# Rounding in small matrix chains on ScalarE, a shorter denominator, three subtractions by transfer, and a new order of the program

## The chip, the core and the metric

The kernel runs on one core of one Trainium2 chip. The metric is the device time of one execution in microseconds (us). The engines are TensorE (PE, with its weight loads shown apart as PEld), VectorE (DVE), ScalarE (ACT), GpSimd (POOL) and SyncE (SP, which here only issues DMAs). Each engine works through its own instructions in order; semaphores join them. A name such as L399 is a line of the kernel before; many operations are recorded in small helpers, so one line can stand for many uses: `mm` (L399) is every matmul, `tt` (L379) every two-tensor operation, `ts` (L383) every tensor with scalars, `stt` (L386) scalar and tensor, `join` (L393) an accumulating DMA from POOL's queue.

## The reference

Two blocks. The first is an attention with sketched polynomial features, for batch 4, 4 heads, 1088 positions, head size 32 and sketch size r = 8:

```python
def phi(x):
    a = np.einsum('rd,bhsd->bhsr', S1, x)
    b = np.einsum('rd,bhsd->bhsr', S2, x)
    return np.einsum('bhsi,bhsj->bhsij', a, b).reshape(*x.shape[:-1], r * r)
q_p, k_p = (phi(q), phi(k))
kv = np.einsum('bhsf,bhsd->bhfd', k_p, v)
z = np.sum(k_p, axis=2)
num = np.einsum('bhsf,bhfd->bhsd', q_p, kv)
den = np.einsum('bhsf,bhf->bhs', q_p, z)[..., None] + 1e-06
return (num / den).astype(np.float32)
```

Its output, as x of shape (4, 1088, 128), goes through the second block, whose large part is the mixing over positions with two 1088 x 1088 matrices:

```python
theta = x @ w_theta
zr, zi = x * np.cos(theta), x * np.sin(theta)
y = np.einsum('ts,bsd->btd', w_tok_r, zr) + np.einsum('ts,bsd->btd', w_tok_i, zi)
u = x + y
return (u + np.maximum(u @ w_ch, 0.0)).astype(np.float32)
```

The denominator can be small beside its summands, so the kernel computes it with more than single precision: values are split into "levels", a part rounded to a coarse grid, whose products are exact, and the rest.

## The kernel before, in words

Everything is written as operations with an engine, a planned duration, and the buffers that they read and write (`op`, `vop`). They are not issued in the order in which they are written: the tuple `ORDER` lists the operations' numbers in the order of issue, and `STARTS` the start times planned for them, from which buffers are assigned to slots and filler matmuls (`spin`, on a tile called idle) are put into planned gaps of PE. So the order on every engine, the SP queue's loads among them, is the search's.

What runs, batch by batch:

- **Loads.** k, q and v of each batch (576 KB each; q of batch 3 in 16 pieces), and 17 rows of the two mixing matrices, in 64-bit words. A row is made into single precision by two ACT passes (L641, L643), a shift (L383) and an add (L379, shown as CUSTOM_DVE) on DVE.
- **Keys** (`key_sums`). A scale comes from the sum of squares (ACT, L691). DVE rounds k to a grid (kb, 16 bit) and takes the rest. PE sums kb by kb, and the rests, into `kk[b]`, 32 x 32 per head. For batches 1 to 3 the second copy of k, on which kb is added, is made by a load and a `join` (the flag `KDMA`): issued by POOL, added in memory by the DMA.
- **Features** (`kfeatures`). PE transposes k, projects it (`sbk`), DVE forms the 8 x 8 products (L379, 128 x 768), and PE sums them with v.
- **Chains** (`chain`, for batch 0, for batch 1, and for batches 2 and 3 together, the tuple `CHAINS`). From the key sums, small matrices on the way to z: `split` rounds the sum into e0 and e1 (three DVE steps and one of ACT), `first` multiplies by the sketch (`sq`, `sf`), `split_t` masks and rounds the result into two levels (DVE and ACT), `second` multiplies by the other sketch (`pbd`), `norm` makes a power of two from a sum over it, and `cut` writes three 16-bit slices into `mv[b]`; `whole` writes the single-precision sum into `mf[b]` on POOL.
- **Query scale and slices** (`query_scale`, `query_slices`). A power of two from the sum of squares of q; q transposed and scaled (ACT, L1029), rounded to 16 bits (h), and the rest f - h in place of f (DVE, 128 x 1152). There is a branch for this last step by ACT and `join`, off for every batch by the flag `QDMA`.
- **Levels and denominators** (`levels`). PE multiplies h by `mv[b]` and f by `mf[b]`; ACT copies the result, `lv` (L1064); a dozen DVE steps make the denominator and scale the numerator's factor.
- **Outputs** (`outputs_x`). DVE forms query products (128 x 768, `g<-lv`), PE transposes them (L1139 for batches 0 and 1), ACT copies (L1143), PE multiplies by kv. Then theta, sine and cosine on ACT, and z on DVE.
- **Mixing.** Batches 0 and 1 row by row; batches 2 and 3 together by a scheme of seven products. PE multiplies z by the rows (`big,zs` in the profile). Then the last projection, a transposition by DVE and the stores.

Of the kernel before, what the change touches and what calls it, by code (L numbers as in the profile page):

```python
# [34 lines left out]
    4, 2, 29, 5, 0, 1, 3, 32, 34, 30, 341, 6, 33, 50, 98, 7, 36, 351, 10, 8, 11, 31, 54, 99, 51, 9, 55, 44, 20, 135,  # L35
    122, 104, 140, 12, 92, 13, 116, 52, 123, 136, 139, 247, 105, 56, 371, 14, 124, 15, 106, 248, 141, 376, 117, 57,
    58, 59, 60, 61, 77, 62, 63, 64, 65, 66, 16, 67, 68, 144, 145, 146, 147, 148, 69, 142, 125, 93, 78, 17, 107, 235,
    254, 79, 35, 108, 308, 236, 80, 342, 100, 25, 258, 126, 312, 70, 53, 313, 260, 202, 344, 310, 26, 343, 261, 311,
    336, 206, 309, 345, 94, 231, 71, 72, 73, 27, 189, 95, 137, 208, 74, 118, 138, 75, 96, 101, 19, 76, 28, 45, 102,
    18, 263, 81, 314, 82, 352, 143, 83, 47, 232, 84, 128, 21, 149, 119, 264, 233, 85, 241, 129, 315, 86, 242, 190,  # L40
    150, 183, 373, 87, 354, 88, 130, 89, 184, 265, 131, 90, 97, 353, 111, 195, 103, 46, 356, 196, 120, 427, 41, 378,
    424, 207, 91, 132, 421, 346, 112, 425, 234, 164, 259, 355, 42, 422, 426, 428, 209, 423, 255, 266, 429, 151, 109,
    152, 165, 430, 110, 328, 377, 243, 431, 153, 166, 154, 244, 155, 156, 386, 191, 337, 432, 326, 433, 324, 329, 157,
    379, 158, 192, 159, 160, 161, 325, 113, 434, 162, 357, 163, 114, 320, 435, 168, 203, 316, 204, 436, 169, 167, 359,
    256, 170, 317, 185, 257, 437, 358, 22, 115, 197, 171, 327, 318, 361, 121, 438, 319, 127, 48, 338, 133, 439, 237,
    262, 339, 249, 172, 366, 447, 198, 134, 347, 440, 450, 448, 250, 173, 454, 186, 238, 49, 443, 321, 174, 380, 441,
    451, 457, 444, 455, 442, 267, 211, 175, 349, 449, 445, 322, 452, 446, 176, 187, 461, 453, 458, 469, 177, 456, 348,
    462, 459, 463, 323, 381, 521, 178, 471, 527, 38, 460, 268, 269, 270, 464, 524, 340, 465, 210, 525, 372, 39, 271,
    23, 212, 522, 472, 467, 360, 477, 466, 179, 473, 272, 273, 468, 274, 479, 275, 213, 276, 528, 526, 205, 480, 180,
    474, 486, 374, 523, 475, 245, 362, 37, 193, 487, 529, 350, 363, 470, 364, 488, 481, 396, 367, 530, 43, 476, 531,  # L50
    277, 278, 279, 214, 188, 199, 215, 280, 216, 217, 218, 219, 220, 489, 281, 483, 532, 383, 365, 478, 482, 221, 369,
    368, 222, 194, 223, 533, 224, 225, 490, 382, 375, 391, 40, 370, 387, 491, 401, 484, 388, 389, 226, 282, 251, 416,
    227, 228, 492, 229, 239, 534, 393, 493, 384, 392, 535, 289, 181, 536, 406, 240, 385, 230, 246, 200, 252, 537, 201,
    494, 398, 182, 394, 538, 403, 495, 390, 290, 402, 539, 287, 397, 496, 411, 540, 288, 253, 554, 541, 543, 395, 542,
    291, 544, 557, 292, 545, 555, 546, 497, 556, 399, 293, 547, 407, 294, 400, 558, 548, 408, 561, 295, 409, 550, 563,
    498, 404, 283, 564, 405, 551, 296, 565, 559, 549, 297, 567, 552, 410, 560, 499, 553, 298, 566, 413, 577, 569, 500,
    330, 571, 299, 417, 485, 572, 331, 562, 573, 300, 658, 579, 284, 574, 661, 568, 659, 304, 301, 662, 285, 660, 580,
    655, 24, 663, 419, 586, 332, 656, 587, 657, 570, 575, 609, 286, 581, 576, 588, 412, 632, 664, 665, 589, 582, 333,
    610, 666, 633, 414, 583, 611, 667, 634, 415, 612, 302, 613, 668, 418, 501, 669, 670, 671, 420, 578, 614, 635, 672,
    502, 584, 673, 334, 636, 303, 515, 590, 585, 509, 516, 503, 688, 637, 591, 504, 681, 592, 510, 682, 638, 305, 615,  # L60
    674, 306, 683, 689, 639, 684, 335, 685, 723, 686, 726, 720, 307, 675, 724, 727, 725, 640, 687, 728, 721, 676, 722,
    729, 641, 677, 730, 678, 616, 679, 680, 593, 847, 705, 731, 690, 706, 732, 617, 691, 733, 692, 505, 693, 694, 734,
    642, 735, 618, 736, 643, 737, 594, 695, 619, 595, 738, 696, 596, 707, 644, 739, 708, 645, 746, 597, 620, 740, 646,
    506, 697, 698, 747, 741, 753, 621, 742, 699, 710, 622, 700, 743, 754, 623, 744, 701, 748, 702, 760, 709, 624, 749,
    745, 842, 750, 703, 625, 751, 704, 712, 752, 626, 755, 711, 627, 598, 756, 757, 713, 774, 758, 714, 759, 817, 767,
    775, 715, 776, 599, 761, 789, 807, 762, 798, 799, 781, 845, 763, 800, 818, 768, 801, 764, 808, 647, 846, 790, 765,
    769, 809, 840, 770, 628, 777, 844, 782, 810, 716, 629, 648, 630, 600, 783, 766, 649, 791, 779, 841, 650, 601, 717,
    784, 792, 718, 786, 793, 507, 771, 508, 802, 772, 811, 778, 812, 785, 773, 517, 813, 837, 819, 780, 803, 848, 787,
    804, 857, 849, 937, 838, 850, 843, 814, 866, 858, 938, 859, 820, 518, 794, 867, 821, 976, 851, 869, 795, 870, 895,
    805, 860, 852, 806, 519, 822, 719, 520, 796, 788, 651, 839, 861, 872, 823, 815, 797, 652, 853, 873, 862, 602, 871,  # L70
    863, 874, 877, 897, 603, 864, 878, 865, 879, 816, 899, 653, 886, 868, 854, 654, 604, 880, 913, 896, 887, 881, 824,
    898, 935, 855, 511, 856, 882, 876, 888, 903, 875, 902, 889, 939, 825, 890, 914, 904, 942, 936, 891, 883, 915, 884,
    940, 905, 885, 916, 900, 892, 827, 893, 941, 948, 894, 906, 944, 933, 949, 934, 901, 907, 512, 605, 826, 943, 908,
    606, 957, 950, 607, 945, 513, 909, 608, 828, 951, 947, 978, 832, 952, 514, 946, 953, 833, 977, 910, 917, 958, 918,
    954, 959, 955, 960, 961, 956, 919, 962, 834, 911, 835, 979, 912, 963, 980, 964, 981, 965, 982, 829, 831, 830, 966,
    920, 631, 921, 989, 990, 922, 923, 967, 983, 971, 984, 972, 991, 924, 985, 968, 986, 973, 925, 975, 974, 987, 992,
    836, 926, 993, 988, 928, 994, 927, 969, 995, 929, 999, 930, 932, 931, 996, 997, 1000, 970, 998, 1001, 1005, 1002,
    1003, 1004, 1006, 1007, 1009, 1008,
)
STARTS = (  # L80
    90, 92, 100, 103, 130, 170, 220, 314, 358, 404, 449, 493, 493, 508, 510, 522, 538, 584, 606, 616, 628, 628, 629,
    630, 644, 657, 669, 696, 703, 706, 708, 741, 840, 749, 774, 781, 807, 814, 832, 840, 850, 855, 870, 878, 982, 888,
    919, 930, 982, 994, 1005, 1252, 1033, 1062, 1064, 1066, 1068, 1070, 1072, 1072, 1074, 1076, 1078, 1080, 1084,
    1093, 1107, 1120, 1122, 1124, 1126, 1128, 1130, 1164, 1179, 1194, 1194, 1198, 1233, 1247, 1248, 1291, 1546, 1336,
    1348, 1355, 1394, 1404, 1408, 1411, 1423, 1468, 1471, 1521, 1522, 1534, 1555, 1583, 1635, 1649, 1682, 1690, 1699,
    1800, 1814, 1826, 1849, 1854, 1863, 1898, 1943, 1956, 1970, 1976, 1996, 2005, 2020, 2028, 2046, 2072, 2073, 2084,
    2108, 2114, 2132, 2152, 2170, 2176, 2195, 2251, 2277, 2287, 2355, 2367, 2389, 2402, 2404, 2423, 2440, 2443, 2455,
    2488, 2505, 2499, 2507, 2537, 2549, 2549, 2570, 2582, 2594, 2613, 2652, 2684, 2699, 2691, 2710, 2720, 2733, 2748,
    2785, 2801, 2828, 2841, 2844, 2845, 2856, 2866, 2890, 2940, 2965, 2979, 3000, 3007, 3020, 3024, 3039, 3060, 3069,
    3085, 3094, 3106, 3114, 3131, 3146, 3149, 3159, 3159, 3181, 3204, 3211, 3266, 3276, 3303, 3313, 3341, 3373, 3371,  # L90
    3375, 3377, 3409, 3424, 3431, 3435, 3439, 3453, 3472, 3481, 3552, 3548, 3559, 3565, 3565, 3572, 3577, 3592, 3588,
    3593, 3655, 3671, 3688, 3698, 3738, 3738, 3744, 3747, 3751, 3757, 3764, 3770, 3784, 3803, 3818, 3844, 3859, 3870,
    3898, 3891, 3928, 3931, 3946, 3973, 3995, 4007, 4029, 4033, 4039, 4044, 4057, 4081, 4092, 4097, 4106, 4121, 4144,
# [56 lines left out]
QTURN = (3,)  # L150
XTURN = (2, 3)
PARTS = ((0, 384), (384, 544))
APOOL = ("4", "3")
KDMA = (False, True, True, True)
RDMA = (False,) * 4
QDMA = (False,) * 4
UDMA = (True, True, False, False)
TILE16, TILE32, TILE64, QUAD = 0.045, 0.12, 0.15, 0.65
ADD_FLY = 9.0
ADD_FLY2 = 3.1  # L160
QFIX = 2.006
NFIX = 1.002
# [141 lines left out]
def act(n):  # L304
    return 0.17 + 0.00083 * n
# [1197 lines left out]
```

## Time and profile before

| what | us |
|---|---|
| median of 3 runs | 226.84 |
| lowest and highest of the runs | 224.06, 228.05 |
| the profiled execution | 224.85 |
| its span, first to last instruction | 223.0 |
| PE busy in it | 212.6 |
| DVE busy | 180.4 |
| ACT busy | 110.9 |
| POOL busy | 56.6 |

The granted clock of TensorE is 0.996 of full speed over the span. A group of the profile reads as: line, engine, operation, what is written from what is read (buffer numbers left out), shapes, count, busy time; `ps` are PSUM banks, `big`, `g`, `sm`, `hf`, `zs`, `lv` classes of buffers by size. The DMAs move 35.90 MB. The 17 rows take a median of 9.9 us from issue to landing, the three joins of keys 10.2.

### The profile page before, as it was taken

How to read it: one execution, taken by the hardware profiler on the slowest of the kernel's cores; microseconds unless marked ns; L12 is line 12 of the kernel's file. 1: busy time of each engine (PE TensorE's matmuls, PEld its weight loads, DVE VectorE, ACT ScalarE, POOL GpSimd, SP SyncE). 2: the span in 40 equal slices, each digit the busy share in tenths (PEclk: the TensorE clock that was granted, in tenths of full speed). 3: DMA queues.
4: the chain of work that ended last, by engine and by line, in shares of the span. 5: the costliest groups of instructions: out<-in, count | busy, mean ns of one | idle time of the engine just before them, and what ended most of it. 6: DMA issues, size and time to landing. Idle time of an engine off the chain costs nothing.

```text
span 223.0 us, 5822 instructions
## 1 busy us (share of the span) xinstructions
PE 212.6 (95%) x2372; PEld 154.2 (69%) x2372; DVE 180.4 (81%) x373; ACT 110.9 (50%) x235; POOL 56.6 (25%) x100
## 2 busy tenths in 40 slices
PE   7888999989999999999999999999999999999990
PEld 7676779786866666768666866677567677667760
DVE  1798999999999999999899589877959946383361
ACT  2899699997979397975822330464640000000000
POOL 1150970223600000044006000010101298990001
PEclk9999999999999999999999999999999999999998
DMA  5999999999967999000004202420450140031446
GB/s 158 392 414 415 414 344 407 418 373 336 245 113 251 332 403 364 11 1 3 0 0 64 39 3 106 110 38 5 171 106 0 29 64 4 0 48 30 71 64 94
DMA packets 30377, 35.90 MB, mean 161 GB/s; under 512 B 23808, under 2 KB 25600, under 8 KB 28176
## 3 DMA queue, kind: packets, MB, share of 16 engines
q1 hardware_dynamic: 24672, 31.51, 41.8%
q0 software_dynamic: 1328, 2.93, 6.4%
q10 hardware_dynamic: 4352, 1.10, 2.5%
q8 instruction: 18, 0.29, 0.5%
q14 instruction: 7, 0.06, 0.1%
HBM read 29.25 MB, written 3.41 MB: 146 GB/s over the span
## 4 chain that ended last, share of the span: by engine, by line
PE 64%; DVE 12%; issue 10%; POOL 5%; ACT 3%; DMA 2%; SPq 1%; POOLq 0%; ACTq 0%
PE ps L399 60%; POOL big L379 5%; DVE big L379 2%; DMA big<-k_l 2%; PE ps L1139 2%; DVE g L379 2%; DVE big L383 1%; DVE lv L379 1%; DVE sm L386 1%; ACT big L691 1%; DVE sm L379 1%; PE ps L1197 1%; PE ps L794 1%; SPq L447 1%; ACT g L797 1%
## 5 line engine op out<-in xcount | busy, mean ns | idle before, releaser
L399 PE MATMUL ps<-big,zs 128*128 128x384 f32 (+2 forms) x380 | 112.1, 437 | 0.0
L399 PEld LDWEIGHTS ps<-big,zs 128*128 128x128 f32 x380 | 66.5, 190 | 33.0 <-issue 0.6
L379 POOL TENSOR_TENSOR big<-big,big 128x544 f32<-128x544 f32 x16 | 22.6, 1464 | 16.0 <-DVE big L379 16.0
L643 ACT ACTIVATE big<-zs 128x1088 int32<-128x1088 uint32 (+1 forms) x18 | 21.0, 1179 | 5.2 <-DMA zs<-w_tok 3.3
L399 PE MATMUL ps<-big,big 128*32 128x32 f32 (+2 forms) x352 | 23.2, 235 | 0.0
L379 DVE CUSTOM_DVE_ANT_0 big<-big,big 128x2176 uint16<-128x2176 uint16 x17 | 21.7, 1278 | 0.7 <-ACT big L643 0.7
L641 ACT ACTIVATE big<-zs 128x1088 f32<-128x1088 f32 x17 | 20.6, 1217 | 0.2 <-DVE big L379 0.2
L399 PEld LDWEIGHTS ps<-big,big 128*32 128x32 f32 (+1 forms) x352 | 15.0, 125 | 6.2 <-issue 1.9
L393 POOL DMA_DIRECT2D g<-big x6 | 5.3, 997 | 52.8 <-ACT g L1284 52.8
L386 DVE SCALAR_TENSOR_TENSOR big<-ps,even,big 128x160 f32<-128x160 f32 (+1 forms) x10 | 5.0, 500 | 14.3 <-PE ps L399 14.3
L431 PE MATMUL ps<-idle 128*128 128x112 bf16 (+1 forms) x70 | 11.4, 316 | 1.3 <-POOL idle L433 1.3
L383 POOL TENSOR_SCALAR mf<-mv 128x32 f32<-128x32 f16 x4 | 1.2, 305 | 45.0 <-DVE mv L383 45.0
L383 DVE TENSOR_SCALAR big<-big 128x1088 int32<-128x1088 int32 x17 | 12.2, 721 | 0.3 <-ACT big L641 0.3
L1284 ACT COPY g<-ps 128x384 f32<-128x384 f32 (+1 forms) x6 | 2.6, 465 | 19.6 <-PE ps L399 19.0
L399 PE MATMUL ps<-sbk,g 128*128 128x64 f32 x72 | 9.9, 279 | 1.2 <-ACT big L1029 0.8
L379 DVE TENSOR_TENSOR g<-lv 128x768 f32<-128x768 f32 x12 | 11.0, 946 | 0.0
L379 DVE TENSOR_TENSOR big<-big,hf 128x1152 f32<-128x1152 f32 x8 | 10.8, 1354 | 0.0
L399 PEld LDWEIGHTS ps<-w,big 128*128 128x128 f32 x72 | 9.3, 191 | 1.7 <-ACT big L1152 0.6
L399 PEld LDWEIGHTS ps<-sbk,g 128*128 128x128 f32 x72 | 8.8, 191 | 2.1 <-ACT big L1029 1.1
L1210 ACT ACTIVATE g<-g 128x384 f32<-128x384 f32 x12 | 6.1, 519 | 7.4 <-DVE g L386 7.4
L399 PE MATMUL ps<-w,big 128*128 128x128 f32 x72 | 9.8, 277 | 0.0
L399 PE MATMUL ps<-mf,big 128*128 128x96 f32 x72 | 9.6, 278 | 0.0
(201 smaller groups left out, 375.6 us busy)
## 6 DMA issues: line engine op xcount, KB each, us to landing
zs<-w_tok SPq DMA_DIRECT2D x17, 1088.0 KB, 9.9
big<-k_l SPq DMA_DIRECT2D x6, 576.0 KB, 10.0
big<-v_l SPq DMA_DIRECT2D x4, 576.0 KB, 8.9
big<-q_l SPq DMA_DIRECT2D x3, 576.0 KB, 10.4
big<-hf POOLq DMA_DIRECT2D x3, 576.0 KB, 10.2
far<-zs SPq DMA_DIRECT2D x2, 576.0 KB, 2.8
zs<-far SPq DMA_DIRECT2D x8, 144.0 KB, 2.9
out<-g SPq DMA_DIRECT2D x24, 48.0 KB, 2.1
```

Source lines behind the costliest of these rows:

```text
L379: eng.tensor_tensor(out=o, in0=a, in1=b, op=f)
L383: (eng or V).tensor_scalar(out=o, in0=a, scalar1=s1, scalar2=s2, op0=op0, **kw)
L386: (eng or V).scalar_tensor_tensor(out=o, in0=a, scalar=s, in1=b, op0=op0, op1=op1)
L393: op("G", 0.9, lambda: G.dma_start(dst(), src(), accum_op=ALU.add), w, r, fly=fly)
L399: T.matmul(o, lhs, rhs, start=start, stop=stop, skip_group_check=True)
L431: T.matmul(nowhere()[:, :n], idle()[:, 0:P], idle()[:, :n], start=True, stop=True, skip_group_check=True)
L447: E.dma_start(dst[i * D:(i + 1) * D, 0:2 * R], s_t.rearrange("d t r -> d (t r)"))
L641: op("A", 0.22 + n * 0.0009, lambda: A.activation(dfn(), words_of(raw(), n)[1].bitcast(F32), AF.Prelu, scale=2.0**-112, alpha=-(2.0**32)), ...
L643: op("A", 0.22 + n * 0.0009, lambda: A.activation(stp(), words_of(raw(), n)[0].bitcast(U32), AF.Copy, scale=2.0**-29), [stp], [raw])
L1139: T.transpose(tr()[:, i * P:(i + 1) * P], qp()[:, i * H + 2 * n:i * H + 2 * n + 2].rearrange("p h i j -> p (h i j)"), ident())
L1210: op("A", act(GW), lambda cs=cs: A.activation(cs()[:, 0], cs()[:, 1], AF.Abs), [(cs, 0)], [(cs, 1)])
L1284: op("A", act(w), lambda: A.copy(u(), yp()[:, :w]), [uT], [yp])
```

## The change

**Chains.** The rounding by adding and subtracting a large number goes from DVE's two-step `stt` to two ACT activations with a bias. e0 is now the rounded first key sum alone (`level`), which is copied out of PSUM as soon as that sum is there (buffer key "s"), e1 the rest of it, and the sum of the rests goes into `first` as a third left operand, e2, copied by ACT:

```diff
-            def split(b=b, t=t, e0=e0, e1=e1):
-                stt(e0(), t()[:, 2], kg[b]()[:, 0:1], kg[b, 0]()[:, 0], ALU.add, ALU.add)
-                stt(e1(), e0(), kg[b]()[:, 0:1], kg[b, 0]()[:, 0], ALU.subtract, ALU.subtract)
-                tt(V, e1(), t()[:, 2], e1(), ALU.subtract)
-            op("V", 0.7, split, [e0, e1], [t, kg[b], kg[b, 0]], lk=1)
-            op("A", act(D), lambda b=b, e0=e0: A.activation(e0(), e0(), AF.Identity, bias=kg[b]()[:, 2:3]), [e0], [kg[b]])
+            def level(b=b, g=g, e0=e0):
+                A.activation(e0(), g()[:, 0], AF.Identity, bias=kg[b]()[:, 0:1])
+                A.activation(e0(), e0(), AF.Identity, bias=kg[b]()[:, 2:3])
+            op("A", 0.4, level, [e0], [(g, 0), kg[b]])
+            vop(D, lambda g=g, e0=e0, e1=e1: tt(V, e1(), g()[:, 0], e0(), ALU.subtract), [e1], [(g, 0), e0], lk=1)
+            op("A", act(D), lambda t=t, e2=e2: A.copy(e2(), t()[:, 2]), [e2], [t])
...
+                for h in range(H):
+                    u = slice(h * D, (h + 1) * D)
+                    mm(tp()[u, n, 1], gs_[b]()[u], sf()[u, 0:R], False, n == nb - 1)
```

In `split_t` likewise: DVE masks, ACT makes the level by two activations a batch, DVE takes the rest in two steps for all batches of the chain. `norm` reads PSUM by ACT instead of DVE and gives one power of two instead of two; `cut` takes seven steps after it for all batches of a chain at once, since the `mv` of a chain's batches now lie in one tile (`mvs`), where it took three and then five a batch:

```diff
-        def norm():
-            a = m4()[:, 1]
-            ts(a, pt(), NFIX, ALU.mult, TINY, ALU.max)
-            ai = a.bitcast(I32)
-            ts(ai, ai, EXPO, ALU.bitwise_and, EXPO, ALU.bitwise_xor)
-            tt(V, nu(), bc(a, 1, [P, 2, nb * H]), bc(ups(), 2, [P, 2, nb * H]), ALU.mult)
...
+        op("A", 0.22, lambda: A.activation(m4()[:, 1], pt(), AF.Copy, scale=NFIX * 2.0**-14, bias=TINY * 2.0**-14),
+           [(m4, 1)], [pt])
...
+            ts(a.bitcast(I32), a.bitcast(I32), EXPO, ALU.bitwise_and, EXPO, ALU.bitwise_xor)
+            tt(V, w_()[:, 0:2], np_().rearrange("p l b (h r) -> p l (b h) r", h=H),
+               bc(bc(a, 1, [P, 2, nb * H]), 3, [P, 2, nb * H, R]), ALU.mult)
...
+            tt(V, a2, a0, a1, ALU.add)
+            rnd(m0, a2, ROUND / 4.0)
+            tt(V, a0, a0, m0, ALU.subtract)
+            tt(V, a1, a0, a1, ALU.add)
+            ts(m1_, a1, UP, ALU.mult)
+            stt(m2_, a1, UP, m1_, ALU.mult, ALU.subtract)
```

`query_scale` reads its sum out of PSUM by ACT (one new activation a batch, one DVE step less).

**Denominators.** The total of the second factor, y, isn't formed any more; the product is split the other way:

```diff
-        vop(2 * NT, lambda: tt(V, fl(0, 2), sl(0, 2), sl(2, 4), ALU.add), [lv], [sx], lk=1)
-        vop(2 * NT, lambda: tt(V, lv()[:, 3:5], bc(sx()[:, 0], 1, [P, 2, NT]), sx()[:, 1:4:2], ALU.mult), [lv], [sx], lk=1)
-        vop(NT, lambda: tt(V, lv()[:, 1], sx()[:, 2], lv()[:, 1], ALU.mult), [lv], [sx], lk=1)
+        vop(NT, lambda: tt(V, lv()[:, 0], sx()[:, 0], sx()[:, 2], ALU.add), [lv], [sx], lk=1)
+        vop(2 * NT, lambda: tt(V, lv()[:, 3:5], bc(sx()[:, 1], 1, [P, 2, NT]), sx()[:, 0:4:2], ALU.mult), [lv], [sx], lk=1)
+        vop(NT, lambda: tt(V, lv()[:, 1], lv()[:, 0], sx()[:, 3], ALU.mult), [lv], [sx], lk=1)
```

**Query rests.** For batches 1 to 3 the branch of `query_slices` that was there takes over: ACT writes -h (16 bits), and POOL issues a DMA that adds it to f in memory.

```diff
-QDMA = (False,) * 4
+QDMA = (False, True, True, True)
```

**Order.** `ORDER` and `STARTS` are new throughout (1028 operations instead of 1010). Of what moves: SP loads q of batch 1 ahead of batch 3's k, and issues four of the 16 pieces of batch 3's q, and the second copies of batches 2's and 3's k, ahead of batch 1's v; DVE rounds batch 1's q ahead of batch 0's denominators, and does three row shifts behind batch 0's first query product that it did ahead of it; PE has 22 fillers of 384 columns instead of 31, all ahead of the first transposes of query products (L1139, in the new file L1132) in both programs.

## The prediction

> **What bounds the kernel now.** I read the slices of the page first, then busy time by stage, then the chain that ended last, then the order of instructions on VectorE (DVE), ScalarE (ACT) and TensorE (PE) in the first 60 us. The slices (5.6 us each):
>
> ```profile
> PE   7888999989999999999999999999999999999990
> DVE  1798999999999999999899589877959946383361
> ACT  2899699997979397975822330464640000000000
> DMA  5999999999967999000004202420450140031446
> ```
>
> Three engines and the DMA are full at once up to about 50 us. After that PE alone never leaves 9. By stage (length; busy time of PE, PEld, DVE, ACT, POOL, each with its instructions; clock; DMA share; GB/s):
>
> ```profile
> 40.00:44.00 4.00, 3.85 (x70) 3.22 (x71) 3.83 (x14) 3.73 (x11) 1.19 (x4) 1.00 1.00 408
> 44.00:48.00 4.00, 3.41 (x93) 3.21 (x85) 3.93 (x10) 4.00 (x10) 1.27 (x1) 1.00 1.04 419
> 48.00:52.00 4.00, 4.00 (x38) 2.83 (x38) 3.93 (x9) 2.82 (x8) 0.00 (x0) 1.00 1.01 318
> 60.00:70.00 10.00, 10.00 (x183) 6.60 (x182) 10.00 (x14) 8.60 (x14) 0.00 (x0) 1.00 0.68 144
> ```
>
> PE has no idle time from 48 us on, until short waits at the very end. The same table for the filler matmuls alone (tile idle) gives 6.4 us of them between 8 and 48 us and none later; PE's plain idle time there adds 2.6. So PE does about 9 us of nothing useful in the front, and 170 us of unbroken work behind it. The chain shows where the one becomes the other (start, length, what):
>
> ```profile
> 45.41 0.71 DVE big L383
> 46.12 0.87 DVE g L379
> 46.99 0.14 issue
> 47.12 0.85 PE ps L1139 x6
> ```
>
> From 8 us the chain is mostly ACT and DVE; at 47.12 the first transposes of batch 0's query products (L1139) start, released by DVE's first product, and from there it stays on PE to 187 us. So **a change pays what it moves 47.12 by, plus what it adds to PE behind it**. The tail of 5.2 us (last matmul end 217.76, span 223.0) is stt, transpose and stores, in both kernels.
>
> **The change, part by part.** In the instruction order of the two programs PE has the same matmuls ahead of its first L1139, but for 8 short ones more (the third set of `first`, batches 0 and 1), 4 of the key sums more, one column sum less and 9 fillers fewer. So I count what DVE and ACT have ahead of that point.
>
> DVE, up to its first product for batch 0, at 46.04:
>
> ```profile
> 25.98 0.25 DVE L386 SCALAR_TENSOR_TENSOR sm<-sm,kg 128x32 f32<-128x32 f32 x1
> 26.27 0.33 DVE L386 SCALAR_TENSOR_TENSOR sm<-sm,kg,sm 128x32 f32<-128x32 f32 x1
> 35.73 0.46 DVE L383 TENSOR_SCALAR big<-lv 128x576 f32<-128x576 f32 x1
> 46.04 2.68 DVE L379 TENSOR_TENSOR g<-lv 128x768 f32<-128x768 f32 x3
> ```
>
> Chains 0 and 1, scales and norm: 21 small instructions go and 9 come. Starts of neighbours lie 0.17 to 0.29 apart, about 0.21: -12 x 0.21 = -2.5. Denominator: one 576-wide sum becomes 288 wide (0.76 to 0.45): -0.3. The searched order puts three row shifts (0.64 from start to start) behind this point, -1.9, and the rounding of batch 1's q before it, +0.7. Sum: **-4.1 us**; DVE's own idle time there (0.72 at 19.9) is small, so alone it could start the products at 41.9.
>
> ACT takes over part of it. Up to the third copy of batch 0's levels it gets the three scaled copies of batch 1's q (L1029, 0.48 each, 1.45), the scaling of w (0.35), two activations with a bias more than now (2 x 0.24), copies of sums for e2 and g (0.3), four small reads of PSUM (0.4) and one 192-wide copy (0.2): **+3.2 us**. Its idle time between 8 us and that copy is 3.7 (0.38, 0.30, 0.55, 0.43, 1.40, 0.27, 0.39). So that copy can't end before 35.2, and ends about where it does now:
>
> ```profile
> 34.22 1.47 ACT L1064 COPY lv<-ps 128x480 f32<-128x480 f32 x3
> 48.50 1.71 ACT L1143 COPY g<-ps 128x384 f32<-128x384 f32 x4
> ```
>
> From there DVE has 46.04 - 35.73 = 10.3 us to its first product; that loses three row shifts (1.92), the short shift-add of w (0.28), a scale (0.17), 0.31 in the denominator and 0.77 in chain 1: 6.9 us. The new order puts a row's add (1.2) ahead of it, which ends some 0.6 us past the level copy, since ACT delivers that row's low half only just before; so the first product starts at 35.7 + 0.6 + 6.9 = 43.2, or 43.4 with the new wait for ACT inside chain 1 (e0 and the levels of `tac`, one in-order step of ACT each, behind a 1.1 us row at worst). ACT up to its first L1143 copy has the same work (two rows, two wide copies and two key scales go, 2.74; the negation 1.08 and the small ones come, 2.74), with 3.9 us of idle to use up: between 44.6 and 48.5. **Front: -2.6 us**, between -4.1 (DVE alone) and 0 (ACT loses what it loses now); I take the sum through ACT since its slack there is 0.5 us.
>
> PE: eight more small matmuls behind the front (batches 2 and 3). Such a set starts 0.1 us before the next instruction, so +0.2.
>
> The transfers. Per batch 1 to 3 a 1152-wide subtraction (1.35, from start to start 1.27) leaves DVE; ACT gets a 1152-wide scaling (about 1.08 without the accumulator read, from L999) and POOL an issue (0.89 to 1.27 in the three joins of keys) with 8.5 to 10.9 us to landing. Two of the three fall where PE is full and DVE no longer decides: nothing gained, and nothing lost while the joins land before the last level matmuls. Batch 1: negated by 39.4 (the level copy, 2.6 us of other ACT work, 1.08), joined 1.1 + 10.9 later, 51.4, wanted by the `mf` matmuls, now at 55.85 and so 8.7 us behind PE's first transposes: 53.2, 1.8 us of cover. On POOL the join stands behind the join of batch 3's keys, which waits for a load; what POOL does for batch 1 (its masks, `mf`) is queued behind it. Price without cover: one for one on PE.
>
> The loads. v of batch 1 is used just before the first L1139:
>
> ```profile
> 43.83 1.21 PE L399 MATMUL ps<-g,big 128*32 128x64 f32 x72
> 80.37 5.75 PE L399 MATMUL ps<-big,zs 128*128 128x384 f32 x18
> ```
>
> Ahead of it in SP's queue stand 11.7 MB now and 13.0 MB in the new order (two more key copies, four of the 16 pieces of batch 3's q): at the 415 GB/s of that stretch 3.2 us later. It is issued at 31.71 behind a row that landed at 37.2, so lands near 38.7 now and near 41.9 then; the small pieces (batch 3's q now comes at 60 to 67 us, where 146 GB/s take a share of 0.70) add up to 0.8, and the join of batch 3's keys, in the new order beside it, 0 to 3. Use by the new pace: 41.2. PE's work from there to L1139 is 1.0. So a landing at 43 costs little: I take +0.2, bounds 0 and 2.5.
>
> Behind 48 us DVE loses three subtractions (3.8), three narrower sums (0.9) and some 19 small instructions of chains 1 to 3 (4.0), and gets the shifted rows (1.2): 7.5 us net, all beside a full PE, worth 0. Sum: -2.6 + 0.2 + 0.2 = **-2.2 us**: 224.85 becomes 222.65 in the profiled execution. That execution was 2.0 below the median of three (226.84), so the forecast for the median is 224.6.
>
> [...] What says that PE is full behind 48 us is the even spacing of its matmuls: 384-wide ones start 0.310 us apart at 80 us (18 in 5.58), 0.305 at 106 and 0.300 at 115; hidden waits come to 144 x 0.007 = 1.0 us at most. [...]
>
> **Rivals.**
> - *DVE alone sets the front* (ACT finds its rows and copies ready and loses its idle time): -4.1 + 0.2, 222.9. For it: the chain names DVE last. Against: ACT's 0.5 us of slack. Chance 0.17.
> - *PE is not full*: it waits unseen for DVE, and the 7.5 us taken from DVE later count as well: 224.6 - 7.5 = 217.1. Against it the spacing. 0.07.
> - *v of batch 1 comes late* (slower): DMA is at a share of 1.0 from 8 to 55 us, and now carries 1.3 MB and a join more ahead of it. From a landing past 46.1 the gain is gone. With the join wholly ahead, 46.4: +0.3 + 0.2, 227.3; with the longest landing seen for an early load (14.9 instead of 10) 4 us more, 231.3. 0.15.
> - *Given back*: ACT stalls in the chains of batches 0 and 1 (four new hand-overs, each behind up to 1.1 us of row), and the front stays where it is: 226.8. 0.06.
> - The forecast, 224.6, from 223.3 to 226: 0.55.
>
> **Numbers.** 2% of 226.84 is 4.5 us, about what a measurement of this kernel can tell from no change: below 222.3 and above 231.4. Faster by that: the second rival, a third of the first, and the low end of the forecast's spread (the three runs shown spread by 4 us): 0.07 + 0.06 + 0.07 = 0.20. Slower: a third of the third rival, 0.05. The rest, 0.75. The range, 221 to 228.5, leaves out the second rival and most of the third's upper half.
>
> **What would show it.** PE's first transposes of query products (now L1132) near 44.5 us, DVE's first product near 43.4, the third level copy near 35.7; ACT without its idle 1.4 us at 24.8; no wait of PE for a DMA of v or for the joins. If the level copy ends at 34 and the transposes start at 43, DVE alone decides; if PE waits for v_l before them, the third rival holds; if PE's unbroken stretch shrinks below 170 us, PE was not full. Wrong in any case if PE shows idle time behind 50 us.

## The result, and the profile after

The changed kernel takes 227.19 us, the median of 22 executions (225.0 to 229.69), the kernel before, in turns with it, 224.78 (22 executions, 224.03 to 228.05): a ratio of 1.0084, 95% interval 1.0056 to 1.0112. It is 0.8% slower; the forecast was 1% faster. The profiled executions went from a span of 223.0 to 226.3 us, at a mean granted clock of 0.996 and 0.975: 3.3 us apart where the medians are 2.4 apart, since the profiled execution of the changed kernel lies 0.9 above its median. Its parts below are those of this execution.

The slices of the page of the changed kernel (5.7 us each; PEclk is the clock that was granted to PE, in tenths):

```profile
PE   7999988699999999999999999999899999999990
DVE  1889988846999999789999499957379758434532
ACT  2999988955998988899450523166250000000000
PEclk9999999856999999999999999999999999999998
DMA  6999999999947995550040141401901012040265
```

Two things are new: PE falls to 6 in the slice from 40 to 45 us, and in the next two slices the clock stands at 5 and 6. In the page of before every slice but the last of PEclk was a 9. Late, from 158 to 164 us, PE has an 8 where it had a 9.

First the part that came as forecast. From ACT's and DVE's order of work, the third copy of batch 0's levels and the first product:

```profile
35.13 0.57 ACT L1057 COPY lv<-ps 128x480 f32<-128x480 f32 x1
...
43.71 1.82 DVE L380 TENSOR_TENSOR g<-lv 128x768 f32<-128x768 f32 x2
```

35.70 and 43.71, forecast 35.7 and 43.4, against 46.04 for the product in the kernel before. So ACT and DVE delivered the 2.3 us. But PE could not use them. From its order of work (start, length, and in brackets the idle time before it with what ended that):

```profile
42.89 0.20 PE L400 MATMUL ps<-hf 128*32 128x32 bf16 x4
45.44 0.87 PE L400 MATMUL ps<-g,big 128*32 128x64 f32 x24 [2.35 <-DMA big<-v_l]
...
47.60 1.54 PE L1132 MATMUL ps<-ident,g 128*128 128x128 f32 x6
```

PE stands still for 2.35 us until v of batch 1 has landed; its first transposes of query products (L1132) start at 47.60, where 44.5 was forecast and 47.12 was the time before. And they take 1.54 us for six, where they took 0.85. The table by stage tells why (length; busy time of PE, PEld, DVE, ACT, POOL; clock; DMA share; GB/s):

```profile
43.00:44.00 1.00, 0.09 (x4) 0.00 (x0) 0.96 (x4) 1.00 (x2) 0.01 (x1) 1.00 1.04 415
44.00:45.00 1.00, 0.00 (x0) 0.00 (x0) 1.00 (x2) 1.00 (x3) 0.91 (x1) 0.55 1.05 374
48.00:50.00 2.00, 2.00 (x12) 2.00 (x11) 0.69 (x2) 1.29 (x4) 0.00 (x0) 0.50 1.03 354
52.00:54.00 2.00, 2.00 (x9) 0.99 (x6) 0.39 (x2) 0.88 (x3) 0.00 (x0) 0.50 1.03 369
54.00:56.00 2.00, 2.00 (x17) 1.63 (x17) 1.71 (x3) 1.68 (x4) 0.00 (x0) 0.92 1.06 442
```

In the middle of PE's idle time the granted clock falls to one half, and it stays there until 54.3 us. PE is busy all the while (2.00 of 2.00), and DVE, which was full here before, now has idle time: it waits for PE, three times for 1.6 us between 46 and 56 us. From 47.60 to 54.3 half of the clock is 3.4 us of PE's work, an estimate from these 6.7 us at 0.50.

Where v was: the chain of waits of the changed kernel, and SP's queue (start and length of the issues):

```profile
31.04 6.41 PE ps L400 x174
37.45 0.28 SPq L715
37.73 0.05 issue
...
37.84 7.47 DMA big<-v_l
45.31 0.14 issue
45.44 2.23 PE ps L400 x73
```

```profile
21.97 10.01 SPq L664 DMA_DIRECT2D big<-q_l  x4
32.09 5.63 SPq L715 DMA_DIRECT2D big<-k_l  x1
37.84 0.86 SPq L672 DMA_DIRECT2D big<-v_l  x2
```

The first four pieces of batch 3's q take SP for 10.0 us and the second copy of batch 3's k for another 5.6. Only behind these is v issued, at 37.84 instead of 31.71, and it lands at 45.3. The chain names PE as what the k copy waited for; the experiments that change that place say otherwise (below).

There is a second stall, late. SP, ACT and PE:

```profile
157.12 0.34 SPq L1162 DMA_DIRECT2D far<-zs  x1
157.52 2.57 SPq L1292 DMA_DIRECT2D out<-g  x4
```

```profile
162.78 0.48 ACT L1277 COPY g<-ps 128x384 f32<-128x384 f32 x1 [4.93 <-DMA out<-g]
```

```profile
163.32 1.86 PE L400 MATMUL ps<-big,zs 128*128 128x160 f32 x9 [1.10 <-ACT g L1277]
```

Four stores of a finished output tile, whose data DVE had ready at 149.6, stand on SP behind the transfer that turns batch 3, which waits for DVE until 157.12. Their tile comes free only at 162.7; ACT needs it for its next copy and waits 4.93 us, and PE waits for ACT for 1.10.

The sum: PE's first transposes 0.48 later than before, and its last matmul ends at 221.59 instead of 217.76. The stretch between them grew from 170.64 to 173.99 us, which 3.4 us of clock and 1.10 of stall more than account for; the rest of PE's work got about 1 us shorter.

### The profile page after: what moved, and what is told of

The parts are those of the page before. It is cut to its first block, busy times and chain, and to the rows that moved or that the text cites. A ratio compares the mean times of both kernels' runs of the same rounds, so it can differ in the third digit from the quotient of the medians.

```text
span 226.3 us, 5847 instructions
## 1 busy us (share of the span) xinstructions
PE 213.7 (94%) x2395; PEld 157.2 (69%) x2395; DVE 170.0 (75%) x337; ACT 117.1 (52%) x258; POOL 58.2 (26%) x101
## 4 chain that ended last, share of the span: by engine, by line
PE 58%; DMA 17%; issue 11%; POOL 6%; ACT 2%; DVE 2%; SPq 1%; POOLq 0%; ACTq 0%
PE ps L400 54%; DMA zs<-w_tok 7%; POOL big L380 6%; DMA big<-v_l 3%; DMA big<-q_l 3%; PE ps L1132 3%; DMA big<-k_l 2%; DMA out<-g 1%; PE ps L1190 1%; SPq L1292 1%; DVE zs L1161 1%; DVE even L1233 1%; ACT zs L1156 1%; ACT big L644 1%; POOL g L394 0%
## 5 line engine op out<-in xcount | busy, mean ns | idle before, releaser
L380 POOL TENSOR_TENSOR big<-big,big 128x544 f32<-128x544 f32 x16 | 21.2, 1353 | 23.3 <-PE ps L400 18.4
L394 POOL DMA_DIRECT2D big<-hf x6 | 6.0, 995 | 49.3 <-ACT hf L1029 36.4
L1057 ACT COPY lv<-ps 128x480 f32<-128x480 f32 x12 | 6.5, 555 | 11.2 <-PE ps L400 11.2
L387 DVE SCALAR_TENSOR_TENSOR g<-g,ps 128x384 f32<-128x384 f32 x12 | 6.6, 547 | 6.5 <-ACT g L1200 6.5
L387 DVE SCALAR_TENSOR_TENSOR big<-ps,big 128x160 f32<-128x160 f32 (+1 forms) x8 | 3.5, 441 | 9.5 <-PE ps L400 9.4
L429 PE MATMUL ps<-idle 128*128 128x112 bf16 (+1 forms) x61 | 9.4, 312 | 1.3 <-POOL idle L431 1.3
L380 DVE TENSOR_TENSOR zs<-zs,g 128x384 f32<-128x384 f32 (+2 forms) x16 | 8.7, 577 | 2.4 <-DMA zs<-far 2.2
L387 DVE SCALAR_TENSOR_TENSOR big<-ps,even,big 128x384 f32<-128x384 f32 (+1 forms) x10 | 4.9, 487 | 7.1 <-PE ps L400 7.1
L1200 ACT ACTIVATE g<-ps 128x384 f32<-128x384 f32 x12 | 5.8, 492 | 7.9 <-PE ps L400 7.8
```

What stands on the lines that cost most here:

```text
L380: eng.tensor_tensor(out=o, in0=a, in1=b, op=f)
L387: (eng or V).scalar_tensor_tensor(out=o, in0=a, scalar=s, in1=b, op0=op0, op1=op1)
L394: op("G", 0.9, lambda: G.dma_start(dst(), src(), accum_op=ALU.add), w, r, fly=fly)
L429: T.matmul(nowhere()[:, :n], idle()[:, 0:P], idle()[:, :n], start=True, stop=True, skip_group_check=True)
L1057: op("A", act(480), lambda g=g, lp=lp: A.copy(lv().rearrange("p l (c n) -> p l c n", n=HR)[:, :, g * GC:(g + 1) * GC], lp().rearrange("p c ...
L1200: op("A", act(GW), lambda cs=cs, th=th: A.activation(cs()[:, 0], th(), AF.Copy, bias=ROUND), [(cs, 0)], [th])
```

## The experiments

Theory A: the loss is the late v, the fall of the clock that PE's idle time brings on, and the late stall; the forecast's gain in the front is there underneath. Its rivals: ACT's hand-overs in the chains or the joins cost the time (B); or v is late because the joins and small pieces take a share of the 16 DMA engines, wherever it stands in the queue (C). Most edits only move operations in the order of issue, after the slots have been assigned:

```diff
+LATER = ((37, 41), (269, 37))     # batch 3's q pieces, then its second k copy, behind v of batch 1
...
         self.order = [self.ops[i] for i in ORDER]
...
+        for i, j in LATER:
+            o = self.ops[i]
+            self.order.remove(o)
+            self.order.insert(self.order.index(self.ops[j]) + 1, o)
```

Line numbers shift by a few in these kernels (L1132 becomes L1135 to L1144).

**v ahead of the pieces and the k copy (e1_v1_ahead).**

> The changed kernel with one edit on SP's queue: v of batch 1 is issued ahead of the first four pieces of batch 3's q and of batch 3's second copy of k. Its slot is free at about 24.5 us (the third transposes of batch 3's k), so it is issued near 24.5 instead of 37.84. Theory A (the loss is the late v and what follows from it): v lands at 42 to 43.5 instead of 45.3, PE waits at most 0.4 us for it, the clock stays at 0.95 or more between 44 and 60 us, the first transposes of query products start at 44.5 to 45.3, and the span is 6 us below the changed kernel's 226.3, near 220. Theory B (the loss is in the chains' hand-overs with ScalarE and in the joins): PE waits in the same place for another engine, and the span stays at 225 to 227. Theory C (it is the transfers' share of the 16 engines that is lost, not the place in the queue): v lands at 45 or later all the same, within 1 us of the changed kernel.

Measured: 222.86 us (4 executions), 0.9918 of the kernel before (0.9892 to 0.9944); span 220.6. Its slices of PE's clock, and PE at the place:

```profile
PEclk9999999999999999999999999999999999999998
```

```profile
42.90 0.54 PE L405 MATMUL ps<-g,big 128*32 128x64 f32 x24
...
44.59 0.94 PE L1137 MATMUL ps<-ident,g 128*128 128x128 f32 x6 [0.42 <-DVE g L385]
```

v is issued at 24.62 and lands 17.8 us later, at 42.4; PE doesn't wait for it, the clock holds, and the transposes start at 44.59. One edit on SP's queue turns 0.8% slower into 0.8% faster. What PE waits for now is DVE's first product, 0.42 us: the path on which the prediction worked out its front. B falls. C falls too in its strong form, since place alone was enough; the next two runs weigh its weak form.

**Only the k copy behind v (e11_second_k_behind).** `LATER = ((269, 41),)`.

> The changed kernel with one edit on SP's queue: only batch 3's second copy of k is issued behind v of batch 1; the four pieces of q stay ahead. Then v takes that copy's place, which waited until 37.7 us for a row issued eight transfers earlier to land. Theory D (each issue on this queue waits for the transfer eight places ahead, and transfers land in order): v is issued at 37.7 again and lands one k copy earlier, 0.576 MB at some 380 GB/s = 1.5 us, near 43.8: PE waits 0.6 to 1.2 us, the clock holds, span 221.5 to 223. Rival (transfers in flight share the engines evenly): v lands at 44.8 or later, PE waits 1.8 us or more.

**The joins of q taken away, the queue left alone (e12_no_q_joins).**

```diff
-            op("A", act(NC * P), lambda: A.mul(hn(), h(), -1.0), [hn], [h])
-            join(f, hn, [f], [hn])
+            op("V", 0, lambda: tt(V, f(), f(), h(), ALU.subtract), [f, hn], [h])
+            op("G", 0, lambda: None, [f], [hn])
```

> The changed kernel with q minus level of batches 1 to 3 on VectorE again (1.3 us each), without ScalarE's negations and the three joins; the order of the loads stays. Only batch 1's join (issued at 40.34) is in flight while v of batch 1 is (37.84 to 45.3). Theory D (place and order in the queue set v's landing): v is issued at 37.7 to 37.9 all the same and lands at most 0.8 us earlier, PE still waits 1.5 us or more, and the first transposes start at 47 to 48. Rival C (the joins' share of the engines made v late): v lands at 43.5 or earlier and PE waits under 0.6 us.

Measured: spans of 221.4 (ratio 0.9897, 0.9829 to 0.9964; 2 executions) and 223.2 (1.0052, 1.0015 to 1.0089; 8 executions). SP and PE of the first, then PE of the second:

```profile
32.36 5.85 SPq L677 DMA_DIRECT2D big<-v_l  x1
```

```profile
44.04 0.54 PE L405 MATMUL ps<-g,big 128*32 128x64 f32 x24 [0.81 <-DMA big<-v_l]
```

```profile
46.20 0.54 PE L400 MATMUL ps<-g,big 128*32 128x64 f32 x24 [2.13 <-DMA big<-v_l]
```

In the k copy's place v is held until 38.2 just as the copy was, though v's own slot is free by 24.6 (the first experiment). So it is the place that is held up, not the buffer. Theory D's reason for it does not hold, though. In the changed kernel the third and fourth pieces start at 24.61 and 28.70, just behind the landings, at 24.60 and 28.69, of the transfers eight places ahead of them. But the row eight places ahead of the k copy had landed at 31.93, before its issue started at 32.09, so the 5.63 us are the issue itself. In e1_v1_ahead, where v is issued ahead of it, the k copy is as slow:

```profile
34.14 5.19 SPq L720 DMA_DIRECT2D big<-k_l  x1
```

What such issues share are the pieces of q, which move in packets of 128 bytes: in the traces of the kernels before and after, each of the six issues on SP of 2 us or more (2.22 to 5.63) has two to four pieces among the eight transfers before it, and no other takes more than 1.84. Why these issues took so long stays open. The transfers slow down as well; before, then after:

```profile
38.00:42.00 4.00, 3.85 (x94) 2.84 (x93) 3.90 (x11) 3.78 (x14) 0.09 (x1) 1.00 1.02 423
38.00:42.00 4.00, 3.90 (x68) 3.60 (x69) 3.09 (x9) 3.88 (x11) 1.48 (x4) 1.00 1.08 299
```

The engines are full in both, but move 299 GB/s instead of 423. Moved one k copy forward, v landed 1.4 us earlier, at 43.9 (forecast 1.5). Without the joins it was issued no earlier (38.87, with all of SP a microsecond later in this execution) and landed at 46.1. So the place in the queue, and what stands ahead of it, set the landing, as theory D forecast; the q joins don't.

The second run also separates the two prices, by chance. PE was idle for 2.13 us and the clock did not fall (1.00 from 44 to 80 us, 0.997 over the span). Its transposes start at 47.40 (47.60 in the changed kernel), its late stall is 0.9 (1.1), and its span is 3.1 us shorter: some 2.7 us are left for the fall of the clock, 3.4 by the sum above.

**The same lateness in the kernel before (e7_before_late_v).** In that kernel `LATER = ((41, 42),)`: v of batch 1 behind batch 2's v.

> The kernel before with one edit: v of batch 1 is issued behind the two copies of k, a row and batch 2's v, so it lands near 46 instead of near 39. Theory A1 (PE's idleness brings the halved clock, in whatever kernel): PE idle 1.8 to 2.6 us at 44 us, clock near 0.5 for several us behind it, first transposes of query products at 48.5 to 49, span 226.5 to 228.5. Rival (the fall of the clock belongs to the changed kernel): the wait alone, span 224.3 to 225 with the clock at 0.99.

Measured: 231.3 us, 1.0268 (1.0209 to 1.0327), span 229.2. PE's clock by slices, PE, and two stages:

```profile
PEclk9999999955999999999999999999999999999998
```

```profile
46.12 2.23 PE L404 MATMUL ps<-g,big 128*32 128x64 f32 x72 [2.28 <-DMA big<-v_l]
50.89 1.49 PE L1144 MATMUL ps<-ident,g 128*128 128x128 f32 x6
```

```profile
44.00:48.00 4.00, 1.88 (x70) 1.85 (x72) 3.91 (x9) 1.96 (x4) 0.37 (x1) 0.81 0.99 365
48.00:60.00 12.00, 12.00 (x81) 10.36 (x71) 6.28 (x18) 6.68 (x16) 0.59 (x3) 0.64 0.62 222
```

A wait of 2.28 us costs this kernel 6.2 us, more than the 3.5 to 5.5 expected: here the half clock also covers the feature matmuls that stand between v's sums and the transposes, so these start 3.8 us later and not 1.6. Nothing of the change is in this kernel; the wait and the clock do it alone.

**Idle matmuls through the wait (e2_cover_wait, e5_cover_again, e6_cover_half).**

```diff
             def sums(g=g, kp=kp):
+                for _ in range(14 if (b, g) == (1, 0) else 0):     # 7 in e6_cover_half
+                    T.matmul(accb()[:, :GW], idle()[:, 0:P], idle(), start=True, stop=True, skip_group_check=True)
```

> The changed kernel with 14 idle matmuls of 384 columns on PE ahead of the first sums of batch 1's values: the wait for v stays, but PE computes nothing useful through it instead of standing idle. Theory A1 (the halved clock from 45 to 54 us comes from PE's 2.35 us of idleness): PE idle under 0.5 us at that place, clock 0.95 or more from 44 to 60 us, first transposes of query products still at 47.2 to 47.8, span 3 to 3.6 us below 226.3, about 223. Theory A2 (the clock falls for another reason, such as the load on the other engines or the transfers): the clock shows the same 0.5 for some 9 us and the span stays at 226 to 227.

> The kernel of e2_cover_wait once more, for an execution at the full clock in the profile: 14 idle matmuls ahead of the first sums of batch 1's values. Theory A1 (the halved clock comes from PE's idleness): clock 0.95 or more from 44 to 60 us, and where the time comes out above 223 all the same, PE's first transposes of query products start later than 47.6 by the difference, so that the idle matmuls themselves are what is paid. Theory A2 (another cause): the clock falls at 44 to 54 us with PE busy.

> The changed kernel with 7 idle matmuls of 384 columns instead of 14 ahead of the first sums of batch 1's values: about 1.2 us of the wait is covered and about 1.2 us is left idle. If the clock falls by the length of one idle stretch, 1.2 us either still brings 0.5 for several us (span 225 to 226.3) or it doesn't (clock 0.95 or more, span 222.5 to 223.5).

Measured: 228.89 us with 14 (1.0159, 1.0124 to 1.0194; without the profiled execution, 272.07 us at a mean clock of 0.754), 229.72 in the repetition (1.0199, 1.0112 to 1.0286; 2 executions), and 226.46 with 7 (1.0058, 1.0025 to 1.0091). PE of e5_cover_again:

```profile
43.26 2.45 PE L817 MATMUL ps<-idle 128*128 128x384 bf16 x14
46.55 0.54 PE L400 MATMUL ps<-g,big 128*32 128x64 f32 x24 [0.84 <-DMA big<-v_l]
...
47.74 0.88 PE L1135 MATMUL ps<-ident,g 128*128 128x128 f32 x6
```

```profile
65.85 7.88 PE L400 MATMUL ps<-big,zs 128*128 128x320 f32 x20 [3.04 <-issue]
```

With PE busy through the wait the clock stays at 1.00 from 44 to 60 us, and with seven (1.78 us idle at the end) it stays too. That agrees with A1, each time in a single profile. But the expected 223 us came in neither kernel, and not because the idle matmuls are paid: the transposes start at 47.74. At 62.8 PE stands still for 3.04 us with nothing that the page names as its cause, and then the clock falls after all, to 0.50 at 66.5 us. The kernel with seven shows 0.6 us of such idle time twice, and its late stall is 1.3. So with the wait covered the clock held here, and the gain was lost further on, to idle time whose cause the traces don't show.

**The late stall (e3_store_ahead, e4_both_moves, e10_both_again).** `LATER = ((783, 526),)`: the turn of batch 3 behind the four stores; then both edits together.

> The changed kernel with one edit late on SP's queue: the four stores of batch 0's first output tile are issued ahead of the transfer that turns batch 3 (issued at 157.12 after a wait for VectorE), not behind it. Theory A: ScalarE's wait of 4.9 us for those stores at 157.8 goes, PE's idle 1.10 us at 162.2 goes with it, and the span falls by 1.1 us, to about 225.2. Rival: the buffers of that size run out one tile later, PE stands idle as long a few us later, and the span stays at 226.3.

> The changed kernel with the edits of e1_v1_ahead and of e3_store_ahead together. Theory A: the gains add, 6 + 1.1, and the span is near 219.2, some 4 us below the kernel before (223.0); PE shows no idle time over 0.5 us from 45 us to its end. Rival: with PE earlier by 5 us the rows of the weights or the outputs of the second phase are late instead, PE waits there, and less than 4 us is left of the sum.

> The kernel of e4_both_moves again, with more rounds, against the kernel before: the ratio is 0.983 again, between 0.978 and 0.988, and the span 219 to 220 with the clock at 0.99 or more. If idle time of PE without a releaser belongs to this kernel too, some of its executions lie 2 to 4 us higher.

Measured: the stores alone 1.0039 (1.0007 to 1.0071; 12 executions), against 1.0084 (1.0056 to 1.0112) for the changed kernel, so 1.0 us, though the intervals overlap; PE's stage from 160 to 170 us goes from 8.90 busy to 10.00. Its span of 223.8 says more than that mainly because in this execution the half clock ended at 51.6 instead of 54.3. Both edits: 221.0 us, 0.9828 (0.9808 to 0.9849), and in the repetition 220.93, 0.9811 (0.9770 to 0.9851), spans 219.2 and 219.3. Waits of PE from 40 us on in e4_both_moves:

```profile
PE ps L1137 <- DVE g L385: 0.5, 1, 0.5
PE ps L405 <- DVE big L385: 0.4, 1, 0.4
```

This version beats both kernels. Its account against the changed kernel closes: 226.3 - 219.2 = 7.1, of which 2.8 are the transposes (47.60 to 44.81), 1.1 the late stall and 3.2 the clock (the stretch from the transposes to the last matmul's end is 169.73 instead of 173.99). And it is steady: six executions of e10_both_again lie within 0.8 us, 22 of the changed kernel within 4.7, with clocks from 0.966 to 0.992.

**VectorE's work given back (e8_dve_work_back, e9_late_dve_work).** In e4_both_moves, y's total again in the denominators, and q minus level on VectorE by the edit of e12_no_q_joins; the second for batches 2 and 3, and the denominators of 1 to 3, only.

> The kernel of e4_both_moves with two parts of the change undone: all four batches compute the denominators with y's total again (VectorE +0.31 us each), and batches 1 to 3 subtract q minus level on VectorE again (+1.3 us each, 5.1 in all, of which 1.6 stand before the first product), without ScalarE's negations (1.08 each) and the three joins. Theory A (PE is full behind 45 us and only what moves its first transposes counts): these start 0.3 to 1.6 us later than in e4_both_moves, and the span is 219.5 to 220.8. Rival (PE is not full, and VectorE's work behind 48 us is paid): 3 to 5 us more, 222 to 224.

> The kernel of e4_both_moves with those parts of the change undone that lie behind 50 us only: batches 1 to 3 compute the denominators with y's total again (VectorE +0.31 us each), and batches 2 and 3 subtract q minus level on VectorE again (+1.3 us each), without ScalarE's negations and without these two joins: 3.5 us more on VectorE. Theory A (VectorE's work behind 48 us is worth nothing): first transposes at 44.8 as in e4_both_moves, no wait of PE for VectorE over 0.5 us, span within 0.7 us of 219.2. Rival (PE waits unseen for VectorE): 2 to 3.5 us more. Idle time of PE that the profile gives no releaser for (2.8 us in e8_dve_work_back) is taken out of the comparison.

Measured: 223.15 us (0.9907, 0.9860 to 0.9954; 10 executions) and 222.29 (0.9861, 0.9806 to 0.9917; 4 executions), spans 223.8 and 219.9. PE of the first, then of the second:

```profile
46.24 0.85 PE L1141 MATMUL ps<-ident,g 128*128 128x128 f32 x6 [1.20 <-ACT big L651]
```

```profile
80.56 1.77 PE L405 MATMUL ps<-big,zs 128*128 128x384 f32 x5 [2.79 <-issue]
```

```profile
45.02 0.96 PE L1143 MATMUL ps<-ident,g 128*128 128x128 f32 x6 [0.53 <-DVE g L385]
```

Work given back in front of the first product is paid: the transposes 1.43 later. (The view names ACT there, but they start 1.10 us behind VectorE's first product, at 45.14, as in e4_both_moves, 43.71 and 44.81.) The other 2.8 us of its span are again idle time without a releaser, which e4_both_moves doesn't have; seven of the ten executions had spans from 220.5 to 222.6. The median is 2.2 us above e4_both_moves, more than the 0.3 to 1.6 that theory A expected; 1.4 of it is at the transposes, and the rest is not assigned. Work given back behind 50 us (VectorE busy 173.2 instead of 169.8 us) cost 0.7 us of span, 0.2 of it at the transposes, and PE's waits for VectorE stay at 0.5 and 0.4. So 3.4 us on VectorE there are worth 0.7 at most, near enough to the prediction's 0; with four executions, one of them at 227.0, it isn't measured closer.

## Why the prediction was wrong

- **Front, -2.6.** Right. Through ACT, 35.70 (forecast 35.7), first product 43.71 (43.4); with v in time the transposes start at 44.6 to 44.8 (44.5). ACT's idle 1.4 us at 24.8 is gone, as forecast. The rival that DVE alone sets the front (41.9) was wrong.
- **PE is full behind 48 us; a change pays what it moves the first transposes by.** Right where PE is fed: the stretch is 169.73 in e4_both_moves, 170.64 before, and 3.4 us of late VectorE work cost 0.7 at most. The eight matmuls more, +0.2, can't be seen in a stretch 0.9 shorter. The tail, taken as 5.2 us in both kernels, is 4.7 in the changed one.
- **The transfers, 0.** Right here: no wait of PE for the join of batch 1's q, and taking the joins out gained v nothing.
- **The loads, +0.2.** This step failed. The text had the queue, the bytes ahead (13.0 MB against 11.7) and the bounds, 0 to 2.5, and then took a landing at 43; it was 45.3. It counted at 415 GB/s, the rate of all queues together; SP's own queue moved 12.21 MB from 10 to 42 us before and 11.02 after, 382 and 344 GB/s, while the joins' queue rose from 0.59 to 1.18 MB. The missing 1.19 MB are 3.5 us at 344. And it did not ask when v is issued: four pieces of 36 KB kept SP from 21.97 to 37.73, with the k copy behind them, where it had "up to 0.8" for these pieces. It also had PE at v by 41.2, where it came at 43.09. So the rival *v of batch 1 comes late* is what happened, at 0.15 and with its point of decision (a landing past 46.1) set too late. That its 227.3 us nearly is the measured 227.19 is luck: it had a landing at 46.4, and neither the fall of the clock nor the late stall.
- **A wait costs PE one for one.** The second failure, one that no rival had: 2.35 us of idle time brought 10.2 us of half clock. That is 3.2 us more behind the transposes and 1.0 ahead of them: from the sums of v to the transposes PE took 2.16 us, and 1.20 at the full clock in e12_no_q_joins. With it the gain was gone from a landing at 45.3.
- **The end of the program.** The stores queued behind the turn of batch 3 cost 1.1 us. The prediction followed the new order of the queues for the front only.
- **Rivals.** *Given back* by ACT's hand-overs: ACT's third copy came on time, and with v in time the gain is there; not so. The time itself, 227.19, lies in the range of 221 to 228.5 and within 2% of before.
- **What would show it.** The prediction named idle time behind 50 us as its refutation. There was one, 1.10 us at 162; the larger fault lay ahead of 50, in the row "no wait of PE for a DMA of v".

## What to carry to other kernels

What stood ahead of v on SP's queue set its landing here: 45.3 us behind the pieces of q and the k copy, 43.9 behind the pieces alone, 42.4 ahead of both. Two things counted: the bytes, at that queue's own rate (344 GB/s), and the time for which the issues ahead keep the issuing engine. Small transfers were not cheap there: four pieces of 36 KB, in packets of 128 bytes, and the copy behind them kept SP for 15.8 us. For the load that PE needs next, count both. Price a wait of PE with the clock behind it: 2.3 us of idle time cost 6 here, in both kernels, when the clock fell, so a load that may be late by two microseconds is worth moving ahead of everything that isn't needed yet. And if an order was searched anew, read every queue to the end, not only in the stage that the change is about.

## What the runs showed of the hardware

- The granted clock of PE fell to 0.50 after idle times of 2.28 (e7_before_late_v, at 46.5 us), 2.35 (changed kernel, 44.1), 3.02 (e3_store_ahead, 44.8) and 3.04 us (e5_cover_again, 66.5), 1.0 to 3.7 us after the idle time began, in two of them only once PE was at work again. It did not fall after 1.78 (e6_cover_half), 2.13 (e12_no_q_joins) and 2.79 us (e8_dve_work_back). In e9_late_dve_work it fell at 28.7 for 3.4 us, with no idle time over 0.4 us between 20 and 29 us. So the length of the idle time alone did not decide it in these runs.
- The half clock lasted 3.4 (e5_cover_again, e9_late_dve_work), 6.8 (e3_store_ahead) or 10.2 us (changed kernel, e7_before_late_v). In e7_before_late_v PE was busy without a break from 47 to 56 us, all of it at a clock of 0.50, so work on PE alone did not bring the full clock back there. What sets the fall and its length, the runs don't show.
- PE stood idle without anything that the page names for 3.04 us in e5_cover_again (from 62.8), for 0.63 and 0.65 us in e6_cover_half (from 43.0 and 77.8) and for 2.79 us in e8_dve_work_back (from 77.8). In e4_both_moves the list of PE's waits has no such time from 40 us on. What PE waited for is not shown.
